# Two channel groups share the second Fourier stage of a long convolution beside a gated MLP, in a new order

## Chip, core and metric

The kernel runs on one core of a Trainium2 chip. The metric is the device time of one execution in microseconds, lower is better. A profile of one execution stands beside the times; the span that it shows runs from the first to the last instruction, and some time lies around it.

The engines in the text: PE (TensorE, matmuls; PEld is its loading of weights), DVE (VectorE), ACT (ScalarE), POOL (GpSimd) and SP, which here only issues transfers (DMAs).

## What is computed

For x = `A_q`, 2048 positions of 640 channels, the result is `x + conv(xn) + mlp(xn)` with `xn` the layer norm of x:

```python
k_shift = sum over t of k_pad[:, t:t+S] * shift_k[:, ks-1-t]       # 4 taps
kv = k_shift * v
y  = irfft(rfft(kv, 2S) * rfft(ssm_k, 2S))[:S] + kv * ssm_D        # per channel, over positions
A  = xn * y
g, u = xn @ w_gate, xn @ w_up                                      # 640 x 1728
B  = (sigmoid(g) * u) @ w_down                                     # 1728 x 640
out = x + A + B
```

## The kernel before

**The MLP.** The 2048 positions are four row blocks (`tr` 0 to 3) of 512. For each, `rec_fc` (matmul at line 751) makes 14 slices `fc` of gate and up, five matmuls of 512 columns for each of the two; ACT takes the sigmoid (line 716), DVE multiplies (lines 719, 722) into `hT`, and some up slices are first copied out of PSUM by ACT. `rec_down` (line 765) multiplies `hT` with `wd` in halves of seven matmuls of 320 columns, and DVE adds the result to `acc` (`fin`, line 771). The normed input comes transposed in `xnT`: for blocks 0 and 1 by PE transposes (line 695), for blocks 2 and 3 by a DMA transpose (line 689) into the same single buffer. For the first two slices of block 0 there is a form that works on one quarter of `xnT0` at a time (`first`, line 732). The statistics of the first four tiles of 128 positions are taken by DVE (tiles 0 and 2) and ACT (tiles 1 and 3: `asum` line 636, `asq` line 642, `asqrt` line 647).

**The convolution.** 640 channels are ten groups (`idx` 0 to 9) of 64: 8 times `JS`, with G = 4 sets of channels side by side on the partitions and two in `b`. The transform over positions is made of two stages with 32 and 64 points:

- `rec_kv`: DVE makes the four-tap product for a group (`tap`, lines 482 and 487, `tt2`, line 488) and multiplies by v (`ttkt`, line 492) into the tile `kvt`.
- `rec_st1` (line 510): 32 matmuls of 64 columns on 32-row strips, once for the filter `ht` (x = 1) and once for `kvt` (x = 0); two evictions each (`ev_T`) into T.
- `rec_st2` (line 530): for each of the 32 values of k, two accumulating matmuls for each 64-row half, with table `Mt` as weights and 64 columns of T (x, j, g) moving; 128 matmuls a group in four blocks of 32, each followed by one eviction `ev_S` into S.
- `rec_prod` (lines 553 to 561): DVE multiplies the spectra, in place in S and in a helper `P`; for groups 3 to 9 one operand is first carried to the other half of the partitions by two DMAs into `P` (line 550, the swap).
- `rec_st3` (line 572): 16 matmuls of 128 columns a group, two evictions (`ev_V`) into VX.
- `rec_st4` (line 602): the last stage, once V of all groups is there, in six units of positions; it uses the buffers of T, S, `kt`, `vt` and `P` again.

**Buffers.** T and S have two buffers each, so that a group is written while another is read. PSUM is eight banks; `c` tiles (all stages of the convolution, `down`) take an aligned pair of banks, `g` tiles (gate and up) one.

**The order.** Nothing is scheduled at run time. The functions record 897 operations with what they read and write; the list `ORDER` gives the sequence in which they are issued, and `ON_DVE` names the evictions that DVE does where ACT could too. Each engine works through its own operations in that order, and waits in front of one whose inputs or buffers aren't ready. SP has its own list of transfers in the same order. Transfers take eight completion counters in turn, and one waits for the transfer that had its counter before.

The functions that the change touches, with their line numbers:

Of the kernel before, what the change touches and what calls it, by code (L numbers as in the profile page):

```python
# [42 lines left out]
def _dft_tables():  # L43
# [74 lines left out]
]  # L118
ON_DVE = [
    48, 98, 100, 135, 136, 137, 139, 142, 144, 146, 147, 427, 469, 474, 485, 492, 799, 804, 809, 865, 867, 868, 872,  # L120
    873, 875, 876, 877, 882, 883, 884, 886, 888, 889, 891, 893, 896
# [106 lines left out]
def kernel(  # L228
# [51 lines left out]


# [25 lines left out]
        "ta": ([P, 2, N2, 2 * JS], BF16), "T": ([P, 2 * K1, 2, JS, G], BF16), "S": ([P, 2, 2, JS, G * K1], BF16),  # L307
        "P2": ([P, 2, JS, G * K1], BF16),
# [5 lines left out]
    def make(b, tag, i):  # L314
# [12 lines left out]
        if tag == "g":  # L327
            if b.startswith("pst"):
                return psh[:, i, 0:NC * P].rearrange("p (c t) -> p c t", c=NC)
            return psa[:, i]  # L330
        shape, dt = SHAPE[tag]
        if b.startswith("kb"):
            shape = SHAPE["ta"][0]
        if b == "Bt":
            shape, dt = [P, N2, 2, N1], U16
# [91 lines left out]
    def load_B():  # L427
        dma(lambda e: e.dma_start(tl["Bt"][:], Bdram.ap()), 128, 8192, w=[("Bt",)], alloc=[("Bt", "T")])

# [65 lines left out]
    def rec_st1(idx, x, first):  # L495
# [6 lines left out]
        T = f"T{idx}"  # L502
        cs = [f"c1_{idx}_{x}_{u}" for u in range(2)]

        def f():
# [388 lines left out]
```

## Time and profile before

| | |
|---|---|
| time, two runs | 243.73 and 246.37 us, median 245.05 |
| the profiled execution | 241.41 us |
| its span | 239.3 us |
| PE busy | 233.4 us, 98%, 3706 matmuls |
| PEld busy | 139.3 us, 58% |
| DVE busy | 189.5 us, 79%, 250 instructions |
| ACT busy | 181.6 us, 76%, 275 instructions |
| moved by DMA | 41.30 MB, mean 173 GB/s |

A group line of the profile gives the line of the kernel, the engine and operation, output and inputs by tile name, their shapes, the count, then after the first bar the busy time and the mean of one in ns, and after the second the idle time in front of them and what ended it. A line of the chain of waits gives start, length and the work that the end of the execution was waiting for at that time. Line 352 and 353 are the helper for evictions on ACT and DVE, so they are told apart by the tile.

### The profile page before, as it was taken

What the parts mean: (1) busy time and instruction counts of PE and PEld (TensorE: products, weight loads), DVE (VectorE), ACT (ScalarE), POOL (GpSimd) and SP (SyncE); (2) the same over time, 40 slices, a digit from 0 to 9 for tenths busy, and PEclk for the clock granted to TensorE, in tenths of its full rate; (3) what the DMA queues carried; (4) which work ended last, traced back from release to release, by engine and by line L of the source; (5) the groups of instructions that cost most, each with busy time, mean ns of one, the idle gap of its engine ahead of it and who ended that gap; (6) DMA issues with size and microseconds to landing.
All of it is one profiled execution on the core that took longest, in us unless ns stands there. A gap on an engine that the chain in (4) does not pass through costs nothing.

```text
span 239.3 us, 8323 instructions
## 1 busy us (share of the span) xinstructions
PE 233.4 (98%) x3706; PEld 139.3 (58%) x3706; DVE 189.5 (79%) x250; ACT 181.6 (76%) x275; POOL 0.7 (0%) x6
## 2 busy tenths in 40 slices
PE   8999999999999999999999999999999999999992
PEld 2754446775446545868664654567675555555672
DVE  2615455199999998999799999999989669769791
ACT  5739989932799999989899999997685864854410
POOL 1000000000000000000000000000000000000000
PEclk9999999999999999999999999999999999999998
DMA  5999999999999429996994938099364859512544
GB/s 157 261 245 245 226 294 228 152 144 147 224 211 187 138 92 234 183 145 102 181 130 108 272 91 258 19 216 238 106 160 138 230 153 298 176 65 60 154 123 113
DMA packets 89115, 41.30 MB, mean 173 GB/s; under 512 B 66800, under 2 KB 85816, under 8 KB 88888
## 3 DMA queue, kind: packets, MB, share of 16 engines
q1 hardware_dynamic: 88168, 39.18, 78.6%
q10 hardware_dynamic: 912, 1.60, 2.2%
q8 instruction: 29, 0.48, 0.9%
q14 instruction: 6, 0.05, 0.1%
HBM read 30.55 MB, written 5.24 MB: 150 GB/s over the span
## 4 chain that ended last, share of the span: by engine, by line
PE 90%; DMA 5%; SPq 2%; ACT 1%; issue 0%; DVE 0%; ACTq 0%
PE psa L751 45%; PE psa L765 26%; PE psa L530 9%; DMA acc<-in_A_q_dram 5%; PE psa L572 4%; PE psa L510 3%; PE psa L602 2%; SPq L399 1%; SPq L374 1%; PE psa L695 0%; ACT VX L636 0%; SPq L396 0%; PE psa L411 0%; ACT sig L716 0%; DVE acc L771 0%
## 5 line engine op out<-in xcount | busy, mean ns | idle before, releaser
L751 PE MATMUL psa<-xnT,w 128*128 128x512 bf16 x340 | 79.3, 379 | 0.0
L765 PE MATMUL psa<-wd,hT 128*128 128x320 bf16 (+2 forms) x448 | 65.6, 299 | 0.0
L765 PEld LDWEIGHTS <-hT 128*128 128x128 bf16 x448 | 42.0, 98 | 17.2
L751 PEld LDWEIGHTS <-w 128*128 128x128 bf16 x340 | 31.7, 98 | 34.8
L352 ACT CAST S<-psa 128x1024 bf16<-128x1024 f32 (+1 forms) x43 | 42.4, 1053 | 7.2 <-PE psa L602 5.0
L751 PE MATMUL psa<-xnT,VX 128*128 128x512 bf16 x180 | 42.6, 379 | 0.1
L716 ACT ACTIVATE sig<-psa 128x512 bf16<-128x512 f32 x52 | 32.2, 634 | 10.0 <-PE psa L751 4.3
L751 PEld LDWEIGHTS <-VX 128*128 128x128 bf16 x180 | 16.6, 98 | 19.0 <-issue 0.4
L352 ACT CAST hT<-psa 128x512 bf16<-128x512 f32 x33 | 20.5, 637 | 8.0 <-PE psa L751 8.0
L352 ACT CAST T<-psa 128x1024 bf16<-128x1024 f32 (+1 forms) x21 | 21.1, 1049 | 2.6 <-PE psa L510 2.2
L530 PEld LDWEIGHTS <-Mt 64*128 64x128 f16 x1280 | 19.6, 95 | 5.3 <-issue 5.1
L492 DVE TENSOR_TENSOR kvt<-ta,vt 128x1024 bf16<-128x1024 bf16 x10 | 21.6, 2159 | 0.2
L530 PE MATMUL psa<-T,Mt 64*128 64x64 bf16 x1280 | 21.6, 190 | 0.0
L771 DVE TENSOR_TENSOR acc<-psa,acc 128x640 bf16<-128x640 f32 (+3 forms) x18 | 13.3, 747 | 9.7 <-PE psa L765 8.9
L355 ACT ACTIVATE T<-psa 128x1024 bf16<-128x1024 f32 x20 | 20.4, 1066 | 0.5 <-PE psa L510 0.5
L722 DVE TENSOR_TENSOR hT<-sig,psa 128x512 bf16<-128x512 bf16 x16 | 10.7, 680 | 12.5 <-ACT sig L716 10.0
L352 ACT CAST VX<-psa 128x1024 bf16<-128x1024 f32 x18 | 18.2, 1042 | 1.8 <-PE psa L572 1.8
L719 DVE TENSOR_TENSOR hT<-sig,hT 128x512 bf16<-128x512 bf16 x36 | 14.5, 420 | 4.9 <-ACT sig L716 4.1
L636 ACT ACTIVATE VX<-acc 128x640 bf16<-128x640 bf16 x14 | 10.2, 732 | 3.4 <-DMA acc<-in_A_q_dram 3.2
L561 DVE TENSOR_TENSOR S<-P 64x2048 bf16<-64x2048 bf16 x10 | 12.2, 1222 | 0.3
L560 DVE TENSOR_TENSOR S<-S 64x2048 bf16<-64x2048 bf16 x10 | 12.2, 1221 | 0.3
L559 DVE TENSOR_TENSOR S<-S 128x2048 bf16<-128x2048 bf16 x10 | 12.2, 1223 | 0.3
(81 smaller groups left out, 210.3 us busy)
## 6 DMA issues: line engine op xcount, KB each, us to landing
w<-in_B_w_up_dram SPq DMA_DIRECT2D x7, 640.0 KB, 7.1
w<-in_B_w_gate_dram SPq DMA_DIRECT2D x6, 640.0 KB, 5.9
P<-S SPq DMA_DIRECT2D x14, 256.0 KB, 3.5
kt<-in_A_k_dram SPq DMA_DIRECT2D x8, 320.0 KB, 6.9
vt<-in_A_v_dram SPq DMA_DIRECT2D x8, 320.0 KB, 7.3
xnd<-VX SPq DMA_DIRECT2D x4, 640.0 KB, 4.5
acc<-in_A_q_dram SPq DMA_DIRECT2D x12, 160.0 KB, 7.6
ht<-in_A_ssm_k_dram SPq DMA_DIRECT2D x8, 192.0 KB, 5.8
```

Source lines behind the costliest of these rows:

```text
L352: fa = lambda: nc.scalar.copy(out=out_fn(), in_=in_fn())
L355: fa = lambda: nc.scalar.activation(out_fn(), in_fn(), ACT.Copy, scale=scale)
L492: dve("ttkt", 1024, lambda: nc.vector.tensor_tensor(out(), f(tl[a][:, 0]), f(tl[vb][:, :, j0:j0 + 2 * JS]), ALU.mult), r=[(a,)] + vr_, w=[ ...
L530: nc.tensor.matmul(tl[c][:, b, 64 * kk:64 * kk + 64], lhsT=Mb[rows, k, 64 - 64 * r:192 - 64 * r], rhs=tl[T][rows, 2 * k + r].rearrange("p ...
L559: dve("pr", 2048, lambda: tt(X(), X(), H(), ALU.mult), r=[(Z, 0), (Z, 1)] + sr, w=[(S_, "p")])
L560: dve("pr", 2048, lambda: tt(X()[0:64], X()[0:64], X()[64:P], ALU.subtract), r=[(S_, "p")], w=[(S_, "z")])
L561: dve("pr", 2048, lambda: tt(X()[64:P], Q()[0:64], Q()[64:P], ALU.add), r=[(S_, "z"), (Z, 0), (Z, 1)], w=[(S_, "q")])
L716: act("sig", 512, lambda: nc.scalar.activation(tl[sg][:], pv(0), ACT.Sigmoid), r=[pk(0)], w=[(sg,)], alloc=[(sg, "sig")])
L719: dve("gmul2", 512, lambda: nc.vector.tensor_tensor(hT[:, fc, :], tl[sg][:], hT[:, fc, :], ALU.mult), r=[(sg,), (hk, fc, 0)], w=[(hk, fc)])
L751: nc.tensor.matmul(tl[c][:], lhsT=w()[:, k, o:o + P], rhs=tl[X][:, k, :], start=(k == 0), stop=(k == NC - 1))
L765: nc.tensor.matmul(tl[p_][:, i, 0:d1 - d0], lhsT=hT[:, fc, t4 * P:(t4 + 1) * P], rhs=wd[:, fc, d0:d1], start=(fc == 0), stop=(fc == NFC - 1))
L771: dve("fin", d1 - d0, lambda i0=i0, i1=i1, d0=d0, d1=d1, m=m, p_=p_: nc.vector.tensor_tensor(acc[:, m, d0:d1].rearrange("p (a d) -> p a d" ...
```

## The change

A pair of groups (2p, 2p + 1) now goes through `st2` in one set of matmuls. T and S are each one constant tile for both groups, with the group index i next to the columns, so that 128 columns (i, x, j, g) move for each table block. A pair has 32 x 2 x 2 = 128 matmuls in eight blocks of 16, again with 1024 elements per eviction; the number of evictions stays. A pair takes both halves of T and of S at once, and the next pair takes them when all their readers are done. The tiles of the last stage that used the slots of T and S are cut out of the joined tiles, and wait for the last `st2` and `st3`. The recording loop goes by pairs, `ORDER` and `ON_DVE` are new lists (44 operations on DVE instead of 36).

```diff
+    TS = 2 * K1 * 2 * JS * G
+    TT = cst.tile([P, 2 * TS], BF16, name="TT")
+    SS = cst.tile([P, 2 * TS], BF16, name="SS")
+    T2 = TT[:].rearrange("p (k i x j g) -> p k i x j g", i=2, x=2, j=JS, g=G)
+    S2 = SS[:].rearrange("p (b i x j n) -> p b i x j n", b=2, i=2, x=2, j=JS)
...
+    def both(n, idx):
+        return [f"{n}{2 * (idx // 2) + i}" for i in range(2)]
...
-    def rec_st2(idx):
-        T, S_ = f"T{idx}", f"S{idx}"
-        tr_ = [(T, x, u) for x in range(2) for u in range(2)]
-        for i in range(4):
-            c = f"c2_{idx}_{i}"
+    def rec_st2(pair):
+        Ts, Ss = both("T", 2 * pair), both("S", 2 * pair)
+        tr_ = [(T, x, u) for T in Ts for x in range(2) for u in range(2)]
+        for i in range(8):
+            c = f"c2_{pair}_{i}"
 
             def f(i=i, c=c):
-                for kk in range(8):
-                    k = 8 * i + kk
+                for kk in range(4):
+                    k = 4 * i + kk
                     for r in range(2):
                         for b in range(2):
                             rows = slice(64 * b, 64 * b + 64)
-                            nc.tensor.matmul(tl[c][:, b, 64 * kk:64 * kk + 64],
+                            nc.tensor.matmul(tl[c][:, b, 128 * kk:128 * kk + 128],
                                              lhsT=Mb[rows, k, 64 - 64 * r:192 - 64 * r],
-                                             rhs=tl[T][rows, 2 * k + r].rearrange("p x j g -> p (x j g)"),
+                                             rhs=T2[rows, 2 * k + r].rearrange("p i x j g -> p (i x j g)"),
                                              start=(r == 0), stop=(r == 1))
...
-            ev("ev_S", 1024, lambda i=i: tl[S_].rearrange("p b x j (g k) -> p b (x j g) k", g=G)[:, :, :, 8 * i:8 * i + 8],
-               lambda c=c: tl[c].rearrange("p b (k n) -> p b n k", k=8),
-               r=[(c,)], w=[(S_, i)])
+            ev("ev_S", 1024, lambda i=i: SS[:].rearrange("p (b n k) -> p b n k", b=2, k=K1)[:, :, :, 4 * i:4 * i + 4],
+               lambda c=c: tl[c].rearrange("p b (k n) -> p b n k", k=4),
+               r=[(c,)], w=[(S_, i) for S_ in Ss])
...
-        sr = [(S_, kb) for kb in range(4)]
+        sr = [(S_, kb) for kb in range(8)]
...
-    for s in range(-1, NI):
-        nx = s + 1
+    for s in range(-1, NI // 2):
+        for nx in (2 * s + 2, 2 * s + 3):
...
         if s >= 0:
             rec_st2(s)
-            rec_prod(s)
-            rec_st3(s)
+            for i in (2 * s, 2 * s + 1):
+                rec_prod(i)
+                rec_st3(i)
```

Parts of the new order, as the engines get them. On PE, after the transposes of all four quarters of block 0 (with the eight `csh` matmuls of line 411 between them), come 17 slices of gate or up of block 0, then the `first` matmuls. After the eight `st2` of pair 1 come 2 `down` halves, `st1` of group 4 (filter), 2 `down` around the small `ck` matmul, 2 `fc`, 4 `down`, `st3` of group 2, `st1` of group 5 (filter), 5 `fc`, `st3` of group 3 with a `fc` between its halves, `st1` of groups 4 and 5 (`kvt4`, `kvt5`), a `fc`, and the eight `st2` of pair 2. Ahead of `st2` of pair 3 stand, at the end, `st3` of group 5, `st1` of group 7 (filter, then `kvt7`) and the last `fc` of row block 2. On DVE, between the products of group 2 and `kvt5` stand 4 products of group 3, the taps of group 5 and six small operations.

More of the change, by code (lines that the diff above doesn't have):

```diff
@@ L330, in make @@
             return psa[:, i]
+        if tag in ("T", "S"):
+            z = (TT, SS)[tag == "S"]
+            if b == "Bt":
+                return z.bitcast(U16)[:, TS * i:TS * i + TS].rearrange("p (n r k) -> p n r k", n=N2, r=2)
+            if b.startswith("xy"):
+                return z[:, TS * i:TS * i + 6 * DM].rearrange("p (y d) -> p y d", y=2)
+            return T2[:, :, int(b[1:]) % 2] if tag == "T" else S2[:, :, int(b[1:]) % 2]
         shape, dt = SHAPE[tag]
@@ L427, in load_B @@
     def load_B():
[L428 removed]
+        dma(lambda e: e.dma_start(tl["Bt"][:], Bdram.ap()), 128, 8192, r=[("T", "free")], w=[("Bt",)], alloc=[("Bt", "T")])
     def load_wd(i):
@@ L501, in rec_st1 @@
         src = [(f"kvt{idx}",)] if x == 0 else [(hb, g) for g in range(G)]
-        T = f"T{idx}"
+        T, T0 = f"T{idx}", both("T", idx)[0]
         cs = [f"c1_{idx}_{x}_{u}" for u in range(2)]
@@ L511, in f @@
                                      rhs=Fb[rows, 0:64], start=True, stop=True, tile_position=(N1 * g, 0))
-        pe("st1", 32, f, r=src + [("A",)] + ([] if first else [(T, "a")]),
-           w=[(c,) for c in cs] + ([(T, "a")] if first else []), alloc=[(c, "c") for c in cs] + ([(T, "T")] if first else []))
+        pe("st1", 32, f, r=src + [("A",)] + ([] if first else [(T0, "a")]),
+           w=[(c,) for c in cs] + ([(T0, "a")] if first else []),
+           alloc=[(c, "c") for c in cs] + ([(t, "T") for t in both("T", idx)] if first else []))
         for u in range(2):
@@ L529, in f @@
                             rows = slice(64 * b, 64 * b + 64)
[L530 removed]
+                            nc.tensor.matmul(tl[c][:, b, 128 * kk:128 * kk + 128],
                                              lhsT=Mb[rows, k, 64 - 64 * r:192 - 64 * r],
[L532 removed]
+                                             rhs=T2[rows, 2 * k + r].rearrange("p i x j g -> p (i x j g)"),
                                              start=(r == 0), stop=(r == 1))
[L534 to L538 removed]
+            pe("st2", 16, f, r=tr_ + [("Mc",), ("M", i // 4)] + ([(Ss[0], "a")] if i else []), w=[(c,)] + ([] if i else [(Ss[0], "a")]) + ([("T", "free")] if (pair, i) == (NI // 2 - 1, 7) else []),
+               alloc=[(c, "c")] + ([] if i else [(S_, "S") for S_ in Ss]))
+            ev("ev_S", 1024, lambda i=i: SS[:].rearrange("p (b n k) -> p b n k", b=2, k=K1)[:, :, :, 4 * i:4 * i + 4],
+               lambda c=c: tl[c].rearrange("p b (k n) -> p b n k", k=4),
+               r=[(c,)], w=[(S_, i) for S_ in Ss])
     def rec_prod(idx):
         S_, Z = f"S{idx}", f"P{idx}"
[L542 removed]
+        sr = [(S_, kb) for kb in range(8)]
         X = lambda: tl[S_][:, :, 0].rearrange("p b j n -> p b (j n)")
@@ L575, in rec_st3 @@
             pe("st3", 8, f, r=[(S_, "z"), (S_, "q"), ("A",)] + ([] if z else [(V, "a")]),
-               w=[(c,)] + ([(V, "a")] if z else []), alloc=[(c, "c")] + ([(V, "VA" if half == 0 else "VB")] if z else []))
+               w=[(c,)] + ([(V, "a")] if z else []) + ([("S", "free")] if (idx, b) == (NI - 1, 1) else []),
+               alloc=[(c, "c")] + ([(V, "VA" if half == 0 else "VB")] if z else []))
             co = 2 * sub * JS + JS * b
@@ L591, in rec_st4 @@
         dma(lambda e: e.dma_start(X(0).rearrange("p (m d) -> p m d", m=n), xnr[:, m0:m1, :]), 128 * n, 1280,
-            r=[("xnd", t) for t in sorted({m0 // 4, (m1 - 1) // 4})], w=[(xb, "x")] + yk, alloc=[(xb, tag)])
+            r=[("xnd", t) for t in sorted({m0 // 4, (m1 - 1) // 4})] + ([("S" if tag == "P2" else tag, "free")] if tag in ("T", "S", "P2") else []), w=[(xb, "x")] + yk, alloc=[(f"xy{v}", tag) for v in ((3, 4) if u == 3 else (u,))])
         cs = [f"c4_{u}_{e}" for e in range(2)]
@@ L825 @@
     rec_first()
-    for s in range(-1, NI):
-        nx = s + 1
-        if nx < NI:
-            rec_st1(nx, 1, True)
-        if nx == 0:
-            rec_kv(0)
-        if nx + 1 < NI:
-            if nx + 1 == NSUB:
-                load_kv(1)
-                load_h(1, 0)
-            if nx + 1 == NSUB + 2:
-                load_h(1, 1)
-            rec_kv(nx + 1)
-        if nx < NI:
-            rec_st1(nx, 0, False)
+    for s in range(-1, NI // 2):
+        for nx in (2 * s + 2, 2 * s + 3):
+            if nx < NI:
+                rec_st1(nx, 1, nx % 2 == 0)
+            if nx == 0:
+                rec_kv(0)
+            if nx + 1 < NI:
+                if nx + 1 == NSUB:
+                    load_kv(1)
+                    load_h(1, 0)
+                if nx + 1 == NSUB + 2:
+                    load_h(1, 1)
+                rec_kv(nx + 1)
+            if nx < NI:
+                rec_st1(nx, 0, False)
         if s >= 0:
             rec_st2(s)
-            rec_prod(s)
-            rec_st3(s)
+            for i in (2 * s, 2 * s + 1):
+                rec_prod(i)
+                rec_st3(i)
     load_B()
```

11 lines of the change are left out of this document (3 added, 8 removed), and 80 rows, old and new, of the table ORDER.

## The prediction

> **What bounds the kernel now.** I read the first lines of the page, then busy time by stretch, then the waits.
>
> ```profile
> span 239.3 us, 8323 instructions
> ...
> PE 233.4 (98%) x3706; PEld 139.3 (58%) x3706; DVE 189.5 (79%) x250; ACT 181.6 (76%) x275; POOL 0.7 (0%) x6
> ```
>
> PE works for 98% of the span, so whatever it loses, in work or in waits, is added to the end. The shares hide a second engine that is almost as full where the Fourier stages run:
>
> ```profile
> 60.00:100.00 40.00, 39.98 (x778) 21.71 (x778) 38.71 (x46) 37.94 (x52) 0.00 (x0) 1.00 0.90 181
> 100.00:140.00 40.00, 40.00 (x795) 25.93 (x788) 37.56 (x38) 37.38 (x48) 0.00 (x0) 1.00 0.86 148
> 140.00:180.00 40.00, 39.97 (x761) 25.63 (x759) 38.36 (x40) 34.55 (x43) 0.00 (x0) 1.00 0.70 165
> ```
>
> The columns after the length are PE, PEld, DVE, ACT. DVE is busy for 114.6 of these 120 us. There it makes the products and the `kvt` tiles, and PE's next `st1` and `st3` need them. The old order is cut so that PE just does not wait:
>
> ```profile
> PEld L510 <- DVE kvt L492: 1.0, 2, 0.5
> ```
>
> One microsecond in all. An order that gives DVE more work, or PE less, in such a stretch makes PE wait.
>
> **The second stage itself.** Pieces of the chain, in order of time (start, length, what):
>
> ```profile
> 102.47 1.08 PE psa L751 x5
> 103.55 0.34 PE psa L510 x32
> 103.90 1.19 PE psa L751 x5
> 105.08 0.95 PE psa L765 x7
> 106.03 0.89 PE psa L572 x16
> 106.93 0.95 PE psa L765 x7
> 107.88 1.97 PE psa L530 x128
> ...
> 117.45 0.57 PE psa L530 x32
> ```
>
> 32 matmuls of `st2` take 0.57 and 128 take 1.97: (1.97 - 0.57)/96 = 14.6 ns for each of 64 columns, two row halves side by side, and 0.57 - 32 x 0.0146 = 0.10 for a switch between tiled and whole-array work (L751 shows it too, 1.19 beside 1.08). A 128-column matmul takes 0.89/16 = 56 ns (L572). After the change 640 matmuls run in 320 pairs; at 56 ns a pair they need 17.8 us, where 1280 x 14.6 ns = 18.7: **-0.9 us**. Bounds: 0, if a pair takes twice the old pair's 29 ns, and -1.3, if it takes what 128 of L765's columns take (0.95/7 x 128/320 = 54 ns). I take -0.9, since L572 has the same width. In the new order the kind of PE work changes 66 times, not 82: 16 x 0.10 = -1.6 us, or half of that if only one side of a change costs it; I take **-1.2**.
>
> [...]
>
> **The start, moved by the new order.** In the old order the first matmuls with weights (`first`, L732) run on a quarter of `xnT0` at a time, as it comes. In the new one 17 blocks of `fc` stand ahead of the first `first`, and each needs all four quarters. ACT's statistics, which these wait for, come later too:
>
> ```profile
> 10.87 1.56 PE L732 MATMUL psa<-xnT,VX 128*128 128x128 bf16 x25
> 12.26 1.24 PE L751 MATMUL psa<-xnT,VX 128*128 128x512 bf16 x5
> ...
> 0.73 1.83 ACTq L374 DMA_DIRECT2D acc<-in_A_q_dram  x4
> ...
> 4.01 0.74 ACT L636 ACTIVATE VX<-acc 128x640 bf16<-128x640 bf16 x1
> ...
> 5.21 0.29 ACT L647 ACTIVATE st<-st 128x1 f32<-128x1 f32 x1
> ...
> 9.22 0.29 ACT L647 ACTIVATE st<-st 128x1 f32<-128x1 f32 x1
> ...
> 11.07 0.69 ACT L352 COPY xnT<-psa 128x640 bf16<-128x640 bf16 x1 [0.70 <-PE psa L695]
> ```
>
> ACT's first `asum` started at 4.01 and its last `asqrt` (L647) ended at 9.51. In the new order the `asqrt` of tile 0, at 5.21 before, stands ahead of that `asum`, and the last load of its tile is third instead of second on ACT's queue, 1.83/4 = 0.46 later. So the `asum` starts at 5.2 + 0.46 + 0.2 = 5.9, and the rest, 5.5 us before less the 0.3 of that `asqrt` and waits of some 0.5, takes 4.7: the last `asqrt` ends at 10.6, not 9.51. From there the old trace needs 2.25 more to the end of the last eviction of `xnT0` (11.76); that one is now on DVE, a little quicker. I put the first `fc` at 12.5. By 12.26, when the old `fc` began, the old PE had done 20, 20 and 25 of its 80 `first` matmuls, 65 x 0.056 = 3.6 us; in the new order these lie ahead still. The eight `csh` matmuls (80 columns, 8 x 56 ns, 0.5) now fill a part of the gap. So 0.2 + 3.6 - 0.5 = **+3.3 us**; bounds 2 and 5. What covered the wait was the work by quarters; PE's queue now holds only `csh` and transposes there.
>
> **The Fourier stretch.** T and S were two buffers each, and one group's products ran while the next group's `st2` was fed. Now a pair fills both, eight `st2` stand nearly in a row, and the products of both groups come after the eighth eviction. I follow DVE from the first product of group 2 to the end of `kvt7` and count what the new order gives it: 17 products, 9 taps, 3 `tt2` (half a tap's elements), 3 `ttkt`, 3 evictions, 11 `gmul` or `gmul2`, 6 small ones.
>
> ```profile
> L352 ACT CAST S<-psa 128x1024 bf16<-128x1024 f32 (+1 forms) x43 | 42.4, 1053 | 7.2 <-PE psa L602 5.0 <-PE psa L530 2.1
> ...
> L352 ACT CAST T<-psa 128x1024 bf16<-128x1024 f32 (+1 forms) x21 | 21.1, 1049 | 2.6 <-PE psa L510 2.2 <-PE psa L602 0.4
> ...
> L492 DVE TENSOR_TENSOR kvt<-ta,vt 128x1024 bf16<-128x1024 bf16 x10 | 21.6, 2159 | 0.2
> ...
> L719 DVE TENSOR_TENSOR hT<-sig,hT 128x512 bf16<-128x512 bf16 x36 | 14.5, 420 | 4.9 <-ACT sig L716 4.1 <-DVE S L561 0.5
> ...
> L482 DVE TENSOR_TENSOR ta<-kt,sT 128x2048 bf16<-128x2048 bf16 x10 | 12.3, 1227 | 0.0
> L559 DVE TENSOR_TENSOR S<-S 128x2048 bf16<-128x2048 bf16 x10 | 12.2, 1223 | 0.3
> ...
> L353 DVE CAST VX<-psa 128x1024 bf16<-128x1024 f32 x2 | 2.4, 1220 | 1.7 <-PE psa L572 1.7
> ...
> 99.11 3.78 ACT L352 CAST S<-psa 128x1024 bf16<-128x1024 f32 x4 [0.48 <-PE psa L530]
> ```
>
> (17 + 9 + 3) x 1.22 + 3 x 2.16 + 3 x 0.61 + 17 x 0.42 = 50.8 us; neighbours overlap a little, small waits add some: 49 to 52, I take 51. In the same stretch of the new order PE has 24 `fc`, 10 half `down`, 7 `st1`, 8 `st3` and 8 `st2` up to the `st1` that needs `kvt7`: 24 x 1.08 + 10 x 0.95 + 7 x 0.34 + 16 x 0.45 + 0.7 for switches = 45.7. DVE cannot start with PE either: five of the eight S evictions are on ACT at 3.78/4 = 0.95, the first 0.45 after PE begins, with part of an `ev_V` (0.4) ahead, so the products start 0.45 + 4.75 + 0.4 - 8 x 0.45 = 2.0 late. PE then waits 51 - 45.7 + 2.0 = 7.3, in two places: some 2 at the `st1` of group 5, the rest at that of group 7. Behind that one stand one `fc` and the pair's `st2`, which needs two T evictions on ACT, 2 x 0.95 against 1.08 + 0.34: 0.5 more. **+7.8 us**; bounds 4 (DVE at 49, products 0.5 late) and 11 (52, and each swap into `P` awaited for 1). What stands behind the waiting `st1` on PE is the last `fc` of row block 2, and with it every `down` of that block that needs its rows. It isn't given back: after that PE has the longer queue again.
>
> The evictions stay 40 of 1024 elements; they now write runs of 4 elements instead of 8. T's evictions write runs of 2 at 1049 ns beside S's 1053, so 0. The products read as many elements as before, 0.
>
> ```profile
> xnT<-xnd SPq DMA_TRANSPOSE x2, 7.7
> ...
> vt<-in_A_v_dram SPq DMA_DIRECT2D x8, 320.0 KB, 7.3
> ```
>
> The load of `xnT2` waits for the last `fc` of block 1. Until the first `fc` of block 2 the new order holds 6 half `down`, 2 `st1` and 2 `st3`, 6 x 0.95 + 0.68 + 0.9 + 0.2 = 7.5, against 7.7 and the issue: **+0.4** (0 to 1). In pair 4 the eight `st2` share four double banks with an `ev_V` and an `ev_u` that are now on DVE: **+0.6** (0 to 1.5). Stage 4 and the stores keep their numbers: 0 (-0.5 to 1).
>
> Sum: -0.9 - 1.2 + 3.3 + 7.8 + 0.4 + 0.6 = **+10.0 us**, so a span of 249.3. The profiled execution took 241.41 for its span of 239.3; the two other runs took 243.73 and 246.37, median 245.05, 3.6 above it. I add to the median: 255.0.
>
> **Rivals.** (1) DVE keeps pace and PE does not wait in the Fourier stretch. The place is `st1` of groups 5 and 7; it decides from a DVE stretch under 45.7 - 2.0 = 43.7 us on. Then the sum is -0.9 - 1.2 + 3.3 = +1.2, so 246.2, not slower by what can be told; with the start covered as well 243. For it: the old order shows 1.0 us of such waits in all. Against: 43.7 needs DVE 14% quicker than its rows. (2) The clock falls in the new gaps.
>
> ```profile
> 1.19 5.27 PE L788 MATMUL psa<-sig 128*128 128x512 bf16 x14 [1.19 <-DVE st L778]
> ...
> 226.34 8.70 PE psa L765 x70
> ...
> 236.00:239.30 3.30, 0.00 (x0) 0.00 (x0) 0.00 (x0) 0.00 (x0) 0.00 (x0) 0.73 0.19 44
> ```
>
> PE ends at 235.04; a mean clock of 0.73 over the last 3.3 us is full speed for 1.5 and half for the rest, so it fell 2.5 us after the last matmul. The new gaps are about 2.5 at the start and over 3 ahead of the `st1` of group 7. Warming again costs what the first 14 matmuls show: 5.27 - 14 x 1.08/5 = 2.2 us each: 257.2 or 259.4. Against: short matmuls stand inside the first gap. [...] (3) SP is late as well: three of the four loads of `vt1` stand behind the swap of group 3 and land 7.3 after issue, about when DVE asks for them: 2 us more on DVE, 257. (4) The change does not do what it says: row halves no longer overlap at 128 columns, 640 x 56 = 36 us, +17: 272. The 14.6 ns speak against it.
>
> **How the numbers follow.** The forecast, 255.0, has a chance of 0.45 (its own range 251 to 258); rival 1 0.17, rival 2 0.22, rival 3 0.10, rival 4 0.03; 0.03 are left for a gain over 2%, for which PE work would have to go that I see stay. Two per cent (4.9 us) is about what a measurement of this kernel can tell from no change. Slower: 0.45 + 0.22 + 0.10 + 0.03 = 0.80; within: 0.17; faster: 0.03. The range goes from 246.5, which holds about half of rival 1, to 262, both falls of the clock with an unknown at its upper bound.
>
> **What would show it.** After the change: `st2` near 17.8 us; the first `fc` at about 12.5 us with no L732 ahead of it; a wait of PE for `kvt` of some 2 us and one of 4 to 6; DVE without gaps between them; PE's share down to 94%; a clock under 1 only if rival 2 holds. The forecast is wrong if the first `fc` starts before 10.5, if PE waits for `kvt` for less than 3 us in all, or if PE stays at 98%.

## The result and the profile after

The changed kernel took 261.94 us, the median of 261.05 and 262.82, against 245.05 (243.73 to 246.37) for the old one, 16.9 us more. The ratio is 1.0787, 95% interval 1.0718 to 1.0857; it isn't the quotient of the two medians (1.069). The ratios leave out executions in a slower state of the chip (in e5 one of 402.1 us at a clock of 0.557, beside 261.5 to 262.7), and 1.0787 stands for an old kernel at 242.8 us, near the 242.2 to 243.5 of all later timings. By it the loss is 19.1 us. Forecast were 255.0 us and slower: the direction was right, the loss of 10.0 us little more than half of what it is. The profiled execution is the one of 262.82, 21.4 us above the profiled one of before.

First lines of the page, the granted clock by slices, and the chain that ended last by engine:

```profile
span 261.0 us, 7030 instructions
...
PE 237.8 (91%) x3040; PEld 142.3 (55%) x3066; DVE 200.6 (77%) x258; ACT 178.9 (69%) x269; POOL 0.7 (0%) x6
...
PEclk9869999999999999999995999968999999999999
...
PE 38%; DVE 28%; DMA 15%; ACT 9%; SPq 4%; issue 3%; ACTq 0%; DVEq 0%
```

PE was the bound in the old kernel (98%). Now the end is reached over PE, DVE, the DMAs and ACT in turn, and the clock falls three times before the end. Busy time by stretch (length, then PE, PEld, DVE, ACT, POOL; clock, DMA share, GB/s), first the beginning of the old kernel, then the new one:

```profile
0.00:20.00 20.00, 18.43 (x147) 10.60 (x148) 6.67 (x22) 11.74 (x26) 0.70 (x6) 1.00 0.91 225
```

```profile
0.00:20.00 20.00, 14.42 (x64) 6.63 (x66) 6.24 (x20) 8.88 (x19) 0.70 (x6) 0.83 0.96 246
60.00:100.00 40.00, 39.22 (x503) 20.23 (x510) 38.91 (x56) 37.93 (x59) 0.00 (x0) 1.00 0.68 148
100.00:140.00 40.00, 35.73 (x505) 24.04 (x508) 37.10 (x36) 28.95 (x36) 0.00 (x0) 0.96 1.02 141
140.00:180.00 40.00, 34.09 (x452) 20.55 (x455) 35.94 (x39) 29.83 (x40) 0.00 (x0) 0.87 0.53 143
```

PE is idle for 5.6 us of the first 20, where the old kernel idled for 1.6; between 60 and 180 us it idles for 11.0, where the old one idled for 0.05. What it waits for (line, releaser: us in all, times, longest), and what DVE waits for most:

```profile
PE psa L524 <- DVE kvt L503: 6.7, 2, 3.5
PE psa L587 <- DVE SS L576: 2.3, 2, 1.2
```

```profile
DVE P L568 <- DMA P<-SS: 9.4, 6, 4.7
```

The start on PE, in order of time:

```profile
7.85 0.45 PE L711 MATMUL psa<-VX 128*128 128x128 bf16 x5 [1.69 <-DVE VX L689]
9.82 0.75 PE L422 MATMUL psa<-kvt,VX 128*128 128x80 bf16 x8 [1.52 <-DMA VX<-dftR]
10.79 2.02 PE L711 MATMUL psa<-VX 128*128 128x128 bf16 x15 [0.23 <-DVE VX L689]
13.49 2.29 PE L767 MATMUL psa<-xnT,w 128*128 128x512 bf16 x5 [0.68 <-DVE xnT L364]
```

The first `fc` starts at 13.49 and takes 2.29 us; the old kernel's five matmuls at 12.26 took 1.24. The three stretches of half clock, 6.83 us each, and the 3.41 us, half as long, just ahead of each:

```profile
10.78:17.60 6.82, 5.85 (x24) 2.90 (x26) 2.21 (x6) 3.10 (x6) 0.00 (x0) 0.50 1.11 300
137.07:143.90 6.83, 5.10 (x85) 3.57 (x88) 5.82 (x6) 3.23 (x4) 0.00 (x0) 0.50 0.33 62
171.20:178.03 6.83, 4.13 (x66) 2.60 (x69) 6.80 (x9) 4.54 (x6) 0.00 (x0) 0.50 0.07 10
```

```profile
7.37:10.78 3.41, 1.20 (x13) 0.83 (x13) 2.14 (x8) 3.35 (x11) 0.00 (x0) 1.00 1.09 236
133.66:137.07 3.41, 1.46 (x44) 0.92 (x41) 2.78 (x4) 3.34 (x5) 0.00 (x0) 1.00 1.08 249
167.79:171.20 3.41, 1.61 (x48) 1.28 (x48) 3.31 (x4) 2.58 (x4) 0.00 (x0) 1.00 0.76 211
```

PE was busy for 5.85 + 5.10 + 4.13 = 15.1 us at half clock. The five matmuls of a `fc` took 2.29 us there and 1.08 at full clock in the old kernel (102.47), so I put that work at half as long at full clock, 7.5 less, an estimate. So the trace adds up: PE ends at 256.26 instead of 235.03, 21.2 later. Its idle time up to there rose by 16.9 (256.26 - 237.76 = 18.5, before 235.03 - 233.4 = 1.6), the half clock adds 7.5, and 3.2 less work is left over. The trace lacks 26 of the 3066 matmuls, all of line 767, and 0.9 us of the idle time lies where such a row has one too few; so 16.0 of idle time and 2.3 of less work are nearer. This is an account of where the time stands in one execution. It doesn't say what comes back when one item is taken away; that is what the experiments are for.

### The profile page after: what moved, and what is told of

Same layout as the page of the kernel before. It is cut to its first block, busy times and chain, and to the rows that moved or that the text cites. A ratio compares the mean times of both kernels' runs of the same rounds, so it can differ in the third digit from the quotient of the medians.

```text
span 261.0 us, 7030 instructions
## 1 busy us (share of the span) xinstructions
PE 237.8 (91%) x3040; PEld 142.3 (55%) x3066; DVE 200.6 (77%) x258; ACT 178.9 (69%) x269; POOL 0.7 (0%) x6
## 4 chain that ended last, share of the span: by engine, by line
PE 38%; DVE 28%; DMA 15%; ACT 9%; SPq 4%; issue 3%; ACTq 0%; DVEq 0%
PE psa L767 19%; PE psa L781 12%; DMA P<-SS 6%; ACT SS L363 4%; DVE kvt L503 4%; DMA acc<-in_A_q_dram 4%; DVE SS L576 3%; DVE SS L575 3%; DVE SS L574 3%; DMA vt<-in_A_v_dram 3%; DVE P L572 3%; DVE SS L364 2%; DMA w<-in_B_w_up_dram 2%; PE psa L545 2%; PE psa L618 2%
## 5 line engine op out<-in xcount | busy, mean ns | idle before, releaser
L767 PE MATMUL psa<-xnT,w 128*128 128x512 bf16 x323 | 80.4, 389 | 2.4 <-DVE xnT L364 0.7
L363 ACT CAST SS<-psa 128x1024 bf16<-128x1024 f32 (+1 forms) x36 | 34.0, 1032 | 4.7 <-PE psa L618 3.2
L363 ACT CAST hT<-psa 128x512 bf16<-128x512 f32 x33 | 19.3, 595 | 10.2 <-PE psa L767 6.0
L363 ACT CAST TT<-psa 128x1024 bf16<-128x1024 f32 (+1 forms) x21 | 20.5, 1021 | 6.1 <-PE psa L524 5.9
L545 PE MATMUL psa<-TT,Mt 64*128 64x128 bf16 x640 | 22.5, 227 | 0.5 <-ACT SS L363 0.4
L363 ACT CAST VX<-psa 128x1024 bf16<-128x1024 f32 x18 | 17.8, 1020 | 6.8 <-PE psa L587 6.7
L366 ACT ACTIVATE TT<-psa 128x1024 bf16<-128x1024 f32 x19 | 19.3, 1043 | 2.8 <-PE psa L524 2.8
L568 DVE TENSOR_TENSOR P<-SS,P 128x2048 bf16<-128x2048 bf16 x7 | 8.6, 1225 | 9.5 <-DMA P<-SS 9.4
L587 PE MATMUL psa<-At,SS 128*128 128x128 f16 x160 | 11.1, 219 | 2.3 <-DVE SS L576 2.3
L587 PEld LDWEIGHTS <-SS 128*128 128x128 bf16 x160 | 9.7, 98 | 5.4 <-DVE SS L576 3.9
L576 DVE TENSOR_TENSOR SS<-P 64x2048 bf16<-64x2048 bf16 x10 | 12.2, 1222 | 0.3
```

The source lines that it names most:

```text
L363: fa = lambda: nc.scalar.copy(out=out_fn(), in_=in_fn())
L366: fa = lambda: nc.scalar.activation(out_fn(), in_fn(), ACT.Copy, scale=scale)
L545: nc.tensor.matmul(tl[c][:, b, 128 * kk:128 * kk + 128], lhsT=Mb[rows, k, 64 - 64 * r:192 - 64 * r], rhs=T2[rows, 2 * k + r].rearrange("p ...
L576: dve("pr", 2048, lambda: tt(X()[64:P], Q()[0:64], Q()[64:P], ALU.add), r=[(S_, "z"), (Z, 0), (Z, 1)], w=[(S_, "q")])
L587: nc.tensor.matmul(tl[c][:, x, 128 * j:128 * j + 128], lhsT=tl[S_][:, x, 0, 4 * b + j, :], rhs=Ab, start=True, stop=True)
L767: nc.tensor.matmul(tl[c][:], lhsT=w()[:, k, o:o + P], rhs=tl[X][:, k, :], start=(k == 0), stop=(k == NC - 1))
```

## The experiments

Each was timed beside the old kernel on the same chip (its medians were 242.2 to 243.5 us), so ratios are compared with 1.0787; 0.004 is about 1 us. With the intervals of both, a difference of less than 2 to 3 us between a variant and the changed kernel isn't shown. The edits are printed shortened.

### What the start, the clock, the waits and the swaps are worth

**The start** (e3, e7, e10): in each, the first part of `ORDER` is that of the old kernel.

```diff
-ORDER = [7, 14, 5, 0, 45, 6, 8, 73, ...    # changed
+ORDER = [6, 0, 7, 4, 8, 5, 16, 13, ...     # old, then changed
```

> The changed kernel with the beginning of the order (to about 40 us) put back as it was in the old kernel: x loads, statistics, the ten first blocks by quarters of xnT0 as they come, then fc; from there on the order of the changed kernel, with the paired st2 and the joined buffers. Theory A, the new start costs 4.3 us of idle TensorE and displaced first blocks and 2.05 us of halved clock, and nothing behind it gives that back: 255.5 us, some 6 below the changed kernel, the first fc near 12.3 us and no fall of the clock before 100 us. Theory B, the later stages wait for loads and for VectorE that come no earlier: 260 us, and the time gained at the start comes back as longer waits near 100 and 210 us.

281.34 us, 1.1563 (1.1475 to 1.1652): far slower, by neither theory. PE's largest waits:

```profile
PE psa L766 <- DMA VX<-in_B_w_up_dram: 9.3, 2, 7.7
PE psa L421 <- DMA kvt<-in_A_shift_k_dram: 6.2, 1, 6.2
```

The old order of PE had got another order of loads; the two belong together. This says nothing on the start itself.

> The changed kernel with the beginning of the order put back as it was in the old kernel, now with the loads up to 50 us spread so that none comes later than its reader asks (in the first try the loads for fc and for the shift came up to 7.7 us late). Theory A, what the new start costs (4.3 us of TensorE and 2.05 us of halved clock) is added to the end: 255.5 to 257.5 us, 4.5 to 6.5 below the changed kernel, first fc near 12.3 us. Theory B, VectorE's stretch takes the time back: 260 us or more.

265.07 us, 1.0881 (1.0783 to 1.0979). ACT's statistics of later rows now waited for their loads, and `sig` and `fc` behind them (3.1 us on PE). Again a miss.

> The changed kernel with the first 165 operations of the old order (to about 45 us: loads, statistics of all rows, first blocks, fc of block 0) word for word, and the rest in the changed order. The two tries before moved loads or statistics so that fc waited for them. Theory A, the 4.3 us of the new start and the 2.05 us of halved clock there are added to the end: 256 to 257 us. Theory B, part of it comes back as waits further on (VectorE, swaps): 258 to 260 us, with kvt7 begun 2 to 4 us sooner than at 171.5.

260.97 us, 1.0745 (1.0704 to 1.0786). PE is busy for 18.66 of the first 20 us, the clock stays full until 169.8, and that fall lasts 3.41 us instead of 6.83. In the account above this is worth 4 us of idle time and two falls and a half, yet the gain is 1 us by the ratio, within the noise, and 3.6 between the profiled executions (259.25). The time lies 1 us above Theory B's range, 4 above A's; `kvt7` starts at 167.95 instead of 171.48, as B said.

**The clock** (e1, e6): matmuls that compute nothing are put where PE waited.

```diff
+            if x == 0 and idx in (5, 7):
+                for _ in range(12):      # e6: 12 for group 5, 4 for 7, and 6 ahead of st3 of group 5
+                    nc.tensor.matmul(tl[cs[0]][:, 0], lhsT=wd[:, 0, 0:P], rhs=wd[:, 0, 0:512], start=True, stop=True)
```

> The changed kernel with matmuls added that compute nothing: 6 more at the very start and 7 ahead of the shift matmuls (L422), 12 ahead of the st1 of group 5 and 12 ahead of that of group 7, each writing a bank that the next real matmul overwrites. They fill the stretches in which TensorE waited (1.7, 1.5, 3.46 and 3.25 us), so no wait for kvt is shorter, but the engine is not idle for long. Theory A, the three falls of the clock (6.83 us at half speed each) are a cost of their own, worked out as 2.05, 2.65 and 2.15 us: no fall before the end, 255 us, some 6.9 below the changed kernel. Theory B, the half speed is hidden behind VectorE, which sets the pace of this stretch anyway, so that the waits for kvt only grow by what the falls no longer take: 260 us, at most 2 below. Either way the start-up of the first fc stays near 13.5 us.

265.33 us, 1.0917 (1.0834 to 1.1000), 3 us slower than the changed kernel, by neither theory. The falls at the start and at 137 us were gone, and group 0's products ended 2.3 us sooner. One fall was left, at 165.84; the 12 matmuls for group 7 then ran at half speed, 5.07 us, and held its `st1` back. In stage 4 PE waited for nothing that the profile shows. From the chain, then from PE in order of time:

```profile
167.94 5.07 PE psa L524 x12
```

```profile
234.91 1.88 PE L623 MATMUL psa<-VX,TT 32*32 32x160 bf16 x171
238.79 0.32 PE L623 MATMUL psa<-VX,TT 32*32 32x160 bf16 x21 [2.00 <-issue]
```

> The changed kernel with fewer matmuls that compute nothing: 12 ahead of the st1 of group 5, 6 ahead of the first st3 of group 5 and 4 ahead of the st1 of group 7; the start is as in the changed kernel. In the first kernel of this kind the 12 ahead of group 7 ran at half speed and held its st1 back by 2.4 us, and TensorE waited 2.7 us in stage 4 for its instructions. Theory A, a halved clock costs what it takes from TensorE: without the falls at 137 and 171 us, 4 to 5 us less than the changed kernel, 257. Theory B, VectorE, ScalarE and the swaps set the pace between 140 and 205 us, so the end of group 7's products comes at most 1.5 us sooner, and the kernel is 0 to 2 us faster, 260.

262.47 us, 1.0805 (1.0734 to 1.0875): no change. The fall at 137 is gone (those at the start and at 170 stayed, the first at half its length), `kvt7` starts at 168.20, the last product of group 7 ends 2.3 us sooner than in the changed kernel, of which 1.1 was there at group 0 already. Then stage 4 lost 1.9 us to `issue`, and after that wait the clock fell there too, for 3.41 us from 237.90 on. Closer to Theory B: full speed in the 7 us from 137 on brought the products about 1 us forward. As the added matmuls may have to do with the new wait in stage 4, e1 and e6 don't show what a fall alone costs at the end.

**The waits for kvt** (e4, e12, e13, e17). In e4 one product and one sum of the taps of groups 5 and 7 are cut to 1 of 64; e12 adds the four loads of `vt1` in one row ahead of the swap of group 3.

```diff
+        n_ = 1 if idx in (5, 7) else N2
-        ... nc.vector.tensor_tensor(tl[a][:], tl[a][:], tl[b][:], ALU.add) ...
+        ... nc.vector.tensor_tensor(tl[a][:, :, 0:n_], tl[a][:, :, 0:n_], tl[b][:, :, 0:n_], ALU.add) ...
```

> The changed kernel with most of VectorE's work on two of the four taps left out for groups 5 and 7 (one product and the sum, on 1 of 64 columns of blocks instead of all): 2.3 us less on VectorE ahead of kvt5 and again ahead of kvt7. The output is not the reference's. Theory A, VectorE's work alone makes TensorE wait: the wait for kvt5 falls from 3.46 to 1.2 us, that for kvt7 from 3.25 to 0, the two falls of the clock go, some 10 us less, 252. Theory B, for kvt5 two things end together: the last load of vt1, which stands behind the swap of group 3 on SP's queue and lands at 136.4 us, holds kvt5 where it was, so its wait stays at 3.4 and its fall of the clock too; only the wait for kvt7 goes: 5 to 6 us less, 256.

258.56 us, 1.0628 (1.0523 to 1.0732), from two executions. Theory B for the waits: that for `kvt5` was 3.26, that for `kvt7` 1.16. Both falls of the clock stayed, 3.41 us long each. PE's wait, and DVE's between 116 and 170 us:

```profile
PE psa L526 <- DVE kvt L505: 4.4, 2, 3.3
...
DVE kvt L505 <- DMA vt<-in_A_v_dram: 2.5, 1, 2.5
```

DVE's 2.3 us ahead of `kvt5` became a wait of 2.5 for `vt1`. Two things end together there. The gain, 3.4 us by the median and 3.9 by the ratio, was less than B's 5 to 6; it is the only gain among the variants that is more than the noise.

> As the kernel with most of two taps left out for groups 5 and 7 (its output is not the reference's), and the four loads of vt1 now stand together ahead of the swap of group 3 on SP's queue. There the wait for kvt5 stayed at 3.3 us, since the last of these loads landed at 135.5. Theory A, that load was all that held kvt5 back: its wait falls from 3.3 to near 1 us and the kernel ends 2 us or more below 258.6. Theory B, VectorE reaches kvt5 no sooner because of the swap of group 3 (its wait grows by what the loads ahead of it take): the wait stays over 2.5 us, 258 us.

264.90 us, 1.0919 (1.0889 to 1.0949): slower, by neither theory. The wait for `kvt5` is gone, and stands now at the `st3` of group 3, since the swap came behind the loads on SP:

```profile
117.71 6.69 SPq L463 DMA_DIRECT2D vt<-in_A_v_dram  x4
124.52 2.79 SPq L566 DMA_DIRECT2D P<-SS  x2
```

```profile
DVE P L569 <- DMA P<-SS: 6.1, 1, 6.1
...
PE psa L588 <- DVE SS L577: 6.1, 2, 5.3
```

So in these two orders SP's queue has no free place for the swap of group 3 and the loads of `vt1`; whichever comes second makes DVE wait.

e13 takes PE's two waits away by the data:

```diff
-        src = [(f"kvt{idx}",)] if x == 0 else ...
+        kv = f"kvt{idx - 1 if idx in (5, 7) else idx}"
+        src = [(kv,)] if x == 0 else ...
```

> The changed kernel; the st1 of groups 5 and 7 read the kvt of groups 4 and 6, which are long there, instead of their own (so these two groups are computed from the wrong rows); VectorE still makes kvt5 and kvt7. TensorE's two waits for kvt, 3.46 and 3.25 us, are gone by the data, and nothing else is touched. Theory A, the waits and the two falls of the clock behind them are lost time of their own: 6.7 and some 4.8 us less, 250.5. Theory B, other work ends nearly as late as kvt (the evictions of T on ScalarE, the st3 whose products VectorE makes later, and then the swaps), so a part of each wait moves to these: 3 to 5 us less, 257 to 259.

259.75 us, 1.0757 (1.0705 to 1.0808): 0.7 us less by the ratio, 2 by the median, within the noise and not 11. In the place of the waits stand others (PE, us in all):

```profile
PE psa L546 <- DVE TT L364: 1.9, 1, 1.9
PE psa L525 <- ACT VX L363: 1.8, 3, 0.7
```

and the clock still fell, at 139.1 and 169.8. The 6.7 us are the place where the loss shows; the waits behind them end nearly as late.

> The changed kernel with the first 165 operations of the old order and, as well, the st1 of groups 5 and 7 reading the kvt of groups 4 and 6. Alone, the first took some 1 to 3.6 us off and the second some 2 to 3. Theory A, the two are separate terms of a sum: 256 to 258 us. Theory B, one floor lies under both (all relieved kernels so far reached the end of the last products at 227.6 to 229.7 us and the end some 29 us later): 259 to 260 us, no better than either alone.

260.02 us, 1.0716 (1.0653 to 1.0780): Theory B by the median. By the ratios the start gave 1.0 us, the waits 0.7 and both 1.7, each within the noise, so whether these two add isn't told. What is told is that both together give 4 us at most, where the account has 4.0 and 6.7 us of idle time for them, with the half clock behind.

**The swaps** (e5, e18):

```diff
-        if idx in SWAP:
-            ... dma(... tl[Z][a] <- tl[S_][o, :, 1] ...); dve("pr", ... tt(Q(), X(), Q(), ALU.mult))
+        if idx in SWAP:
+            ... dve("pr", 2048, lambda a=a, o=o: tt(Q()[a], X()[a], H()[o], ALU.mult))   # two halves
```

> The changed kernel, same order, but no swap DMA in any group: where the two halves of S were swapped into P by two DMAs and one product of 128 partitions followed, two products of 64 partitions now read the other half directly, as groups 0 to 2 do already. VectorE gets one product more (1.24 us) in each of seven groups, 8.7 us in all; SP loses 14 DMAs. Theory A, VectorE's work is what makes TensorE wait: 5 to 9 us slower, 268. Theory B, the pair's chain is made of latency: both groups' products wait for the eighth eviction, the one buffer P takes the swap of the second group only when the first group's products are done, and each swap takes 5 us from issue to product; without them VectorE's 9.4 us of waits on swaps go and the pairs follow each other sooner: 3 to 6 us faster, 257.

262.15 us, 1.0785 (1.0701 to 1.0868): no change at all, so neither theory.

> The changed kernel without swap DMAs once more, for its profile (its time was 261.5 to 262.7, neither of the two theories). If the 9.4 us of VectorE's waits on swaps are gone and 8.7 us of products stand in their place, the two cancel on VectorE; the waits of TensorE for kvt are then about as long as before, 6 to 7 us in all, with the end at 260 to 263.

260.82 us in its one execution, as expected for two effects that cancel: DVE is busy for 208.9 instead of 200.6 us and has no wait for a swap. PE's waits for `kvt` went down to 4.4, not the 6 to 7 expected, and those at `st3` up:

```profile
PE psa L524 <- DVE kvt L503: 4.4, 2, 3.3
PE psa L593 <- DVE SS L582: 3.2, 2, 2.1
```

### The columns, and the order without pairs

> The changed kernel, same order and same joined buffers, but each st2 matmul of 128 columns is two of 64. Theory A, what counts is the columns and a small share for each matmul (14.6 ns a matmul in the old trace): 1280 x 14.6 = 18.7 us against 17.6, so 0.5 to 1.1 us slower, less where the evictions set the pace of st2. [...] Theory C, two row halves overlap worse at 128 columns than at 64: faster.

```diff
-    nc.tensor.matmul(tl[c][:, b, 128 * kk:128 * kk + 128], ..., rhs=T2[rows, 2 * k + r], ...)
+    nc.tensor.matmul(tl[c][:, b, 128 * kk + 64 * h:128 * kk + 64 * h + 64], ..., rhs=T2[rows, 2 * k + r, h], ...)   # h in 0, 1
```

268.22 us, 1.1034 (1.0940 to 1.1128): 6 us above the changed kernel. 96 matmuls of 64 columns take 1.57, 16 ns each, near Theory A's 14.6, so no better overlap of the two row halves. But the rows of `st2` broke off:

```profile
109.97 1.57 PE L544 MATMUL psa<-TT,Mt 64*128 64x64 bf16 x96
...
114.26 3.18 PE L544 MATMUL psa<-TT,Mt 64*128 64x64 bf16 x128 [1.92 <-issue]
```

```profile
PE psa L544 <- issue: 5.5, 4, 2.4
```

5.5 us of waits for nothing that the profile shows, in a kernel of 640 matmuls more. Theory A's 1.1 and these come to 6.6, near the 6; that is a sum again and no test.

e9 takes the old kernel's operations, each group for itself, in the changed order (only `ORDER` and `ON_DVE` differ from the old kernel).

> The old kernel's operations (st2 for one group at a time, 64 columns, T and S of their own, a group's products free to start after its own four evictions) in the order of the changed kernel: where that has the eight st2 and evictions of a pair, here stand the four of the first group and then the four of the second. Theory A, the loss lies in the order: 260 to 264 us, as slow as the changed kernel, with the long waits for kvt5 and kvt7 and the falls of the clock where they were. Theory B, the loss lies in the pairing (products that wait for eight evictions, one wait for both groups): 245 to 252 us.

273.60 us, 1.1264 (1.1229 to 1.1299). Theory A, and more than that: in this order the kernel without pairs is slower than with them by 11.7 us.

```profile
PE psa L529 <- issue: 6.4, 4, 2.2
PE psa L509 <- DVE kvt L491: 5.5, 2, 3.3
```

The waits for `kvt` are there without any pair. The old operations lose 31 us in the new order; in it the pairs win 11.7 back, and among what the kernel without pairs has more are 6.4 us of waits for `issue`.

> The paired kernel in the old order, changed as little as the pairs demand: an operation stays in its place of the old order unless what it reads is not yet made, or its buffer not yet free, and then it comes at the first place where it can. So the st2 of a pair stand where the second group's stood, and products, swaps and st3 of the first group behind them. Theory A, pairs do not fit the old order: TensorE waits 7 to 11 us for the products of each pair, 295 to 310 us, so some new order was needed and its costs belong to the pairs. Theory B, the old order holds pairs as well: 245 to 255 us, and the whole loss was the choice of the new one.

311.74 us, 1.2833 (1.2723 to 1.2943). Theory A. PE's and DVE's largest waits:

```profile
PE psa L586 <- DVE SS L575: 30.3, 5, 8.8
...
DVE P L567 <- DMA P<-SS: 49.8, 4, 17.9
```

In the old order the products of a pair come too late for each `st3` on PE, and DVE waits 50 us for swaps. The pairs need another order, and its costs belong to them.

Whether one without the loss exists: e8 and e14 are orders for pairs, e11 and e15 orders for single groups, found by exchanging operations against the measured durations (`ORDER` and `ON_DVE` alone).

> The paired kernel, nothing changed but the order of its operations and which of ScalarE and VectorE does an eviction: TensorE work that is ready is put ahead of the st1 and st3 that wait, VectorE makes kvt5 and kvt7 sooner, and no stretch of waiting is long enough for the clock to fall. Theory A, the loss lies in this order and its long waits, not in the pairs: close to the old kernel, 245 to 250. Theory B, the pairs themselves cost: a group's products start only after eight evictions instead of four, S has no second buffer, so the waits are spread but not gone (worked out over the measured durations: some 20 us of short waits where the old order has 4): 253 to 258 us, still 10 us or more above the old kernel.

> The paired kernel with the old order's first 165 operations and a new order behind them, chosen so that it stays short when a load lands up to 3 us late or TensorE is 1% slower. Theory A, the order was the loss and pairs can follow as closely as single groups: 243 to 248 us. Theory B, with pairs VectorE, ScalarE and the swaps of two groups come in one piece and leave TensorE some 20 us of short waits in any order: 252 to 258 us.

> The old kernel, nothing changed but the order and which engine does an eviction, found by trying exchanges against the measured durations. It bounds how much an order alone can still give without pairs: 239 us if the short waits of the old order (2 to 3 us) go, 250 and more if loads at the start come late, as they did in the reordered pairs.

> The old kernel with only the order behind its first 190 operations changed, chosen in the same way as that of the reordered pairs. It tells what the same choosing gives without pairs: 238 to 242 us if its short waits go, 243 and more if the order gives nothing more.

e8 277.01 us, 1.1407 (1.1309 to 1.1504); e14 269.40, 1.1138 (1.1074 to 1.1201); e11 262.00, 1.0812 (1.0744 to 1.0879); e15 254.94 in its fastest execution and 259.43 to 261.10 in the three others. All four miss. e11 and e15 are 13 to 20 us slower than the old order of the very same operations, so this way of choosing is worse than the order it began with, and e8 and e14 prove nothing against pairs. That question stays open.

## Why the prediction was right and wrong

The mechanism was right: in the new order PE waits at the start and for `kvt5` and `kvt7`. Two steps failed. DVE's stretch was put at 51 us with next to no waits of its own, and took 57.4. The clock was put at nothing in the sum, and fell three times. In the terms of the account above, the forecast had 3.9 us too little idle time on PE (12.1 for 16.0) and nothing for the 7.5 of the half clock; the work was right (2.1 less for 2.3). Behind both lies a premise, that whatever PE loses is added to the end; the experiments don't bear it out for this order.

- **st2's columns, -0.9: right.** In the trace after, 48 matmuls of 128 columns take 1.51 and 32 take 1.07:

```profile
110.70 1.51 PE L545 MATMUL psa<-TT,Mt 64*128 64x128 bf16 x48
...
180.23 1.07 PE L545 MATMUL psa<-TT,Mt 64*128 64x128 bf16 x32
```

  (1.51 - 1.07)/16 = 27.5 ns, 55 a pair, 17.6 us in all for the 17.8 forecast. With the fewer changes of kind, -1.2, the forecast was 2.1 us less work; 2.3 is what the account leaves. What it did not see is that 640 instructions fewer also spare waits for `issue` where `st2` stands in long rows: in this order 5.5 to 6.4 us (e2, e9).
- **The start, +3.3: the idle time about right, +4.0** (5.58 against 1.57 in the first 20 us). The first `fc` was 1 us later than said, 13.49, since the first rows came later than said. DVE's first statistics, before and after:

```profile
4.05 0.89 DVE L629 BATCH_NORM_STATS2 VX<-acc 128x6 f32<-128x320 bf16 x2 [2.91 <-DMA acc<-in_A_q_dram]
```

```profile
5.64 0.89 DVE L645 BATCH_NORM_STATS2 VX<-acc 128x6 f32<-128x320 bf16 x2 [4.17 <-DMA acc<-in_A_q_dram]
```

  That is 1.6 us, where the prediction allowed 0.46 for the loads; the `asum` came at 7.02 instead of 5.9, the last `asqrt` ended at 11.33 instead of 10.6. `csh`, counted as work that fills the gap, waited for its table until 9.82, but the transposes behind it had to wait for DVE until 10.79 anyway.
- **The Fourier stretch, +7.8: DVE's work right, its waits left out.** From the first product of group 2 to the end of `kvt7`:

```profile
116.23:173.63 57.40, 47.81 (x594) 28.40 (x598) 50.86 (x53) 39.50 (x52) 0.00 (x0) 0.92 0.68 142
```

```profile
DVE P L568 <- DMA P<-SS: 1.6, 2, 0.8
DVE hT L735 <- ACT sig L732: 1.5, 2, 1.2
DVE kvt L503 <- DMA vt<-in_A_v_dram: 0.6, 1, 0.6
```

  DVE's busy time is 50.86, forecast 50.8. But the stretch takes 57.4, not 51: 6.5 us in which DVE itself waits. "Small waits add some" was the step that failed here, and "DVE without gaps" on the list of signs. The two waits of PE came at the two `st1` named, 3.46 and 3.25 us for 2 and 5.3; their sum, 6.7 for 7.3, was close, but by luck: the prediction's own formula gives 57.4 - 45.7 + 2.0 = 13.7 for a stretch of 57.4. PE was idle for 9.6 us of it and busy for 47.8, longer than forecast, as it ran at half clock for a part. Two waits at `st3` (2.3) and short ones came on top, so PE idles for 11.0 between 60 and 180 us.
- **The clock, 0 in the sum: the largest term that it left out.** It fell three times, and 7.5 us stand in the trace's account for it. That 10.0 + 7.5 comes near the 16.9 between the medians is luck: the ratio says 19.1, the account 21.2, and how much comes back without the falls isn't shown. Rival 2 had the mechanism and two places, at 2.2 us each; in the account they are 2.9, 2.6 and 2.1, and the wait ahead of the `st1` of group 5, which I had put at 2 us, was a third. I had read the fall as something that needs 2.5 us of idleness, from the end of the old trace alone. The new trace shows something else. All distances between the changes of its clock up to 178.03 us are whole multiples of 3.413 us: 137.07 - 10.78 is 37 times that, 171.20 - 137.07 ten times, each stretch of half clock two. And PE was not idle in the 3.41 us ahead of the falls, but busy for 1.20, 1.46 and 1.61. The old trace could have told it: its clock fell at 237.53, 2.5 us after the last matmul, so 0.91 us of the 3.41 ahead of that fall were busy. The measurement decides: 1.61 us busy of 3.41, 47%, did not keep the clock up.
- **That the terms can be added** is what the sum assumed, and the experiments don't bear it out. By the ratios, taking away the start with two falls of the clock gave 1.0 us, PE's waits for `kvt` 0.7, both together 1.7, the fall at 137 nothing, the swaps nothing; only less work for DVE gave more than the noise, 3.9. A sum that comes near the time is no proof of its terms. One thing does go with the time: DVE's last product (group 9) ends at 231.86 us in the changed kernel, 227.64 in e10, 228.01 in e4 and 234.11 in e12, and the span ends 29.0 to 30.0 us after it in these, in e2, e3, e7, e13, e17 and e18. Only in e1 and e6, which wait for `issue` in stage 4, it is 31.5 and 31.6. So what a variant won or lost stood when DVE's products were done. My reading is that DVE, the swaps, the loads on SP and ACT's evictions end within 1 to 3 us of each other on the way there, so that whatever is freed meets the next; the waits that took each other's place in e4, e12, e13 and e18 show it for these four.
- **Rival 3** (loads of `vt1` late behind the swap) had the place right and the price too high: DVE waited 0.6 us for them in the changed kernel, not 2, and 2.5 once it was quicker (e4). **Rival 1** fell with the 6.7 us of waits for `kvt`. **Rival 4** fell at 27.5 ns. PE's share, 91%, was forecast as 94%; the prediction's own terms give 93 (231.3 of 249.3 us).
- **Pairs or order.** The prediction put its terms at the pairs' buffers and at the new order without telling them apart, and the runs don't part them either. The new order costs the old operations 31 us (e9) and the pairs cost 68 in the old one (e16), yet both together cost 19. So the pairs are not the loss in this order; whether a better one exists for them is open.

## What to carry to other kernels

Here an order that left almost no wait on one engine was worth more than the saving for which it was rewritten; cost a new order as a whole, with each engine's own waits and its loads, before the work that is saved. Where an engine falls from 98% to about 90% busy, look for stretches like the three here, 3.41 us with TensorE busy for 1.20 to 1.61, price the half clock behind them (7.5 us in this account), and ask what else ends at the same time. And test a sum by taking terms away one at a time and two together: where several engines end close to each other, a term alone may bring back little.

## What the hardware did that I had not expected

In the trace of the changed kernel the clock stood at 0.50 of full speed from 10.78 to 17.60, from 137.07 to 143.90 and from 171.20 to 178.03 us; the distances from one of these changes to the next, 6.83, 119.47 and 27.31 us, are 2, 35 and 8 times 3.413 us. Cut into stretches of that length, the trace has PE busy for 35, 43 and 47% of the one ahead of each fall, and for 65% or more of every other one at full speed before PE's end. The clock rose after stretches of 93, 100 and 94% and stayed down after 78, 49 and 27%. In the old trace PE was busy for 27% of the stretch ahead of its one fall, at 237.53. Counted in the same way over 15 traces, of the changed kernel and its paired variants (all but e5), 44 falls came before PE's end: 42 followed a stretch in which PE was busy for at most 51%, the other two 59% and 66%. Seven stretches at full speed with 44 to 50% passed without a fall. The clock stayed down for 3.41 to 13.65 us; it rose after stretches of 79 to 100%, and stayed down after some of up to 85%.

PE stopped in rows of its own matmuls. Rows of many short ones (64-column `st2`, `st4`) broke off for up to 2.4 us at a time with `issue` as the only reason (longest 2.0 in e1, 2.4 in e2, 1.9 in e6, 2.2 in e9); the 64-column rows of the old kernel, at most 128 matmuls, did not. What PE waited for there isn't shown. That these are loads of code is only my reading: in e1 the instruction queue moved 16 KB from 236.5 us on, next to the wait of 2.00 us that ended at 238.79, and no run here took such loads away.
